# First block of a fused attention and expert kernel: state scaled by a kept copy, more load buffers, one unit issued later

## The chip, the core and the metric

The kernel runs on one core of a Trainium2 chip. The metric is the device time of one execution in microseconds (us); lower is better. In the profile TensorE is PE (matmul) and PEld (weight load), VectorE is DVE, ScalarE is ACT, GpSimd is POOL, and SyncE is SP, whose queue (SPq) issues nearly all DMAs here.

## What is computed

```python
f = 1 / (1 + exp(-f_logit))
for t in range(768):                      # 4 batches x 8 heads, head size 48
    state = f[t][:, None] * state + k[t] (outer) v[t]
    y[t] = q[t] @ state
x = y, heads side by side                 # 3072 tokens x 384
h = x @ w_in                              # 384 -> 2048
x = (h * clip(h + 3, 0, 6) / 6) @ w_out   # 2048 -> 384
e = argmax(x @ w_gate)                    # one of 8 experts for each token
out = gate * sigmoid(x @ w_output_gate)[e] * (relu(x @ w1[e]) @ w2[e])   # 384 -> 1024 -> 384
```

w_in and w_out arrive as 64-bit floats, the rest as 32-bit floats.

## The kernel before

Tokens are worked on in 8 blocks of 384. For each block four attention **units** (two batch-head pairs of a block of tokens each, `attention(blk, pr, xx)`) write a quarter of the tile `xx` that the first multi-layer product (`mlp`) of that block reads. A unit turns the recurrence into products: DVE runs two scans (`gg` L233, the running decay, and `r0` L235, its inverse) and four elementwise steps (`rg` L237, `kt` L238, `kb` L240, `qt` L242); PE transposes `kb` (`pk` L248) and multiplies (`pa` L253, `pkv` L266); DVE masks (`at` L260) and adds states (`st` L274 to L277 in the first half of a sequence, L281 in the second); ACT copies the states (`sbd` L284); PE multiplies again (`py` L291, L294); ACT and DVE write the result in two parts (L300, L301). The fourth unit of a block writes into `yx`, which six DMAs (L305) spread over `xx`; only then can the products `ph` of that block (L310 to L312) start.

`mlp` takes 16 hidden tiles f. For each it does nine products into `ph` (two PSUM buffers), the activation (ACT L347, DVE L348, ACT L349, DVE L350; the buffer of `ph` is free after L348), and two tiles later nine products into `acc` (L323 to L325).

Before and during block 0 the 64-bit weights are converted in 24 **parts** (`split64`): a DMA of 512 KB into `raw` (two buffers; the tile's name in the profile), then DVE L138, L140, ACT L143, DVE L144, ACT L145, DVE L146. Seven parts are issued between the units of block 0, the others two per hidden tile of block 0.

Which unit is issued where is set by `UNITS = (-5, 0, 5, 9)` and the function `between(f)`, called after each hidden tile f: the first unit of block 1 (the fifth unit) is issued ahead of block 0's `mlp`, the first unit of a later block at f = 11 two blocks ahead, the three others at f = 0, 5, 9 of the block ahead. Program order is only a priority: a scheduler with a timeline of its own sets the order of the instructions on each engine (last line of the file), and each engine then works strictly in that order, SP's queue of DMAs too. Eight products on zeros (`keep_warm`) stand in the units of block 0.

Buffers: `qt` and `xt` 3, `kt` 2, `vs` 2, `th`, `gg` and `r0` 1. A load into a buffer waits until its last reader is done. In program order `gg` of a unit is read last by L277, which scales the new state by the last column of `gg`; L244 copies the same column to `gcmin`.

After the last block the tokens are gathered by expert and run through eight experts (`up`, `down`, `rows_in`, `rows_out`); this part is not touched.

Of the kernel before, what the change touches and what calls it, by code (L numbers as in the profile page):

```python
# [10 lines left out]
F32 = mybir.dt.float32  # L11
F32R = mybir.dt.float32r
BF16 = mybir.dt.bfloat16
I32 = mybir.dt.int32
U32 = mybir.dt.uint32
# [7 lines left out]
P = 128  # L23
# [3 lines left out]
KD = DM // P  # L27
FF = 2048
NF = FF // P
# [3 lines left out]
TB = 384  # L33
NB = NT // TB
CH = 128
# [13 lines left out]
def fused(ctx: ExitStack, tc: tile.TileContext, q, k, fl, v, vt, w_in, w_out, wg, w1, w2, out):  # L49
# [79 lines left out]
    def split64(pool, hi, lo, src):  # L129

        raw = work.tile([P, SW // 2, 2], U32, tag="raw", name="raw64")
        loads.append(nc.sync.dma_start(out=raw.rearrange("p n t -> p (n t)"), in_=src))
        lw, hw = raw[:, :, 0], raw[:, :, 1]
# [18 lines left out]
    def load_first(pool, i, wih, wil, woh, wol):  # L152

        wohf, wolf = (t.rearrange("p f d -> p (f d)") for t in (woh, wol))

        def up(kt):
            sl = slice(i * 512, (i + 1) * 512)
            split64(pool, wih[:, kt, sl], wil[:, kt, sl], w_in.bitcast(U32)[:, kt, 1024 * i:1024 * (i + 1)])

        def down(j):  # L160
            sl = slice(j * 512, (j + 1) * 512)
            split64(pool, wohf[:, sl], wolf[:, sl], w_out.bitcast(U32)[:, 1024 * j:1024 * (j + 1)])

        return [partial(up, kt) for kt in range(KD)] + [partial(down, j) for j in range(3 * i, 3 * i + 3)]
# [47 lines left out]
    def attention(blk, pr, xx):  # L212
# [4 lines left out]
        kt = at2.tile([R, NCH, CH], F32, tag="kt", name="kt")  # L217
# [25 lines left out]
        gend = fl2(gg)[:, TB - 1:TB]  # L243
        nc.scalar.copy(gcmin[:, n:n + 1], gend)  # L244
# [17 lines left out]
        if blk == 0:  # L262
            keep_warm(1, fl2(kb))
# [4 lines left out]
        if blk == 0:  # L268
            keep_warm(1, fl2(kb))

        if half == 0:
# [5 lines left out]
            nc.vector.tensor_scalar_mul(state[pr][:, 0, :], st[:, 0, :], gend)  # L277
# [183 lines left out]
    parts = [part for i in range(NF // 4) for part in load_first(cv, i, *wfirst)]  # L461
# [5 lines left out]
    for pr in range(4):  # L467
        if UNITS[pr] < -1:
            att_unit(1, pr)
# [158 lines left out]
    for blk in range(NB):  # L628
# [11 lines left out]
        def between(f):  # L640
# [6 lines left out]
            for pr in range(4):  # L647
                if f == UNITS[pr] and blk + 1 < NB:
                    att_unit(blk + 1, pr)
                if f == UNITS[pr] + NF and blk + 2 < NB:  # L650
                    att_unit(blk + 2, pr)
# [64 lines left out]
    with tc.If(general > 0):  # L716
# [41 lines left out]
        with ExitStack() as es:  # L758
            gp = es.enter_context(tc.tile_pool(name="gw", bufs=1))
            wg1 = first_weights(gp)  # L760
            for i in range(NF // 4):
                for part in load_first(gp, i, *wg1):
                    part()
# [105 lines left out]
```

## Time and profile before

| | us |
|---|---|
| three runs | 864.46, 866.75, 869.58 |
| median | 866.75 |
| profiled execution | 864.98 |
| its span on the engines | 863.3 |
| PE busy in it | 805.9 (93%) |
| DVE busy in it | 526.4 (61%) |

The profiled execution is 1.77 us under the median, and its span leaves 1.7 us around it. PE is busy nearly all the time from about 75 us on. Before that, in the units of block 0, it mostly waits. The shares over the whole span hide that DVE is busy all the time in just this stretch. Matmuls overlap in the records: a row's time is 0.33 us at the full clock, but the next one starts 0.17 us later. DVE's rows overlap a little too, so the step from one start to the next is the price.

### The profile page before, as it was taken

Reading aid. Unit: us, or ns where it says so; the run is one execution under the profiler, and the core shown is the slowest. Engines: PE = TensorE matmul, PEld = TensorE weight load, DVE = VectorE, ACT = ScalarE, POOL = GpSimd, SP = SyncE. Lnnn points to the kernel's source line nnn. Section 1 sums busy time; section 2 is a strip of 40 time slices with the busy share of each in tenths; the row PEclk is TensorE's granted clock in tenths of the full one; section 3 lists DMA queues with packets and bytes.
Section 4 is the critical chain, followed back from the end, with each engine's and each line's share of the span. In section 5 each row is a group of like instructions: output and inputs, shape, how many; then the busy total and the mean of one; then the engine's idle time right before and its main releaser. Section 6 shows DMA issues by size and latency. Waiting matters only on the chain.

```text
span 863.3 us, 14521 instructions
## 1 busy us (share of the span) xinstructions
PE 805.9 (93%) x5503; PEld 746.4 (86%) x5503; DVE 526.4 (61%) x1118; ACT 396.4 (46%) x843; POOL 62.3 (7%) x103
## 2 busy tenths in 40 slices
PE   7558998999998999999899999999999999999995
PEld 3338987998997998999799899899898999999994
DVE  6999975569554578654567843463464452554631
ACT  5556654447434455633445533453354342453520
POOL 2000000200010010010010010010100011101111
PEclk9558999999999999999999999999999999999998
DMA  6565495023021113110211200050254163255600
GB/s 200 169 187 156 153 283 168 29 68 106 1 70 52 31 62 92 48 61 26 65 63 42 57 29 11 14 174 20 68 178 157 34 207 131 92 185 183 216 26 28
DMA packets 42412, 85.01 MB, mean 98 GB/s; under 512 B 5954, under 2 KB 29795, under 8 KB 42333
## 3 DMA queue, kind: packets, MB, share of 16 engines
q1 hardware_dynamic: 39052, 74.50, 28.5%
q0 software_dynamic: 3280, 9.49, 3.0%
q8 instruction: 45, 0.74, 0.4%
q14 instruction: 35, 0.28, 0.1%
HBM read 65.77 MB, written 16.26 MB: 95 GB/s over the span
## 4 chain that ended last, share of the span: by engine, by line
PE 47%; DVE 4%; DMA 3%; ACT 2%; issue 1%; SPq 0%; POOL 0%; POOLq 0%; DVEq 0%; ACTq 0%
PE ph L310 7%; PE ph L312 7%; PE ph L311 7%; PE acc L323 3%; PE acc L324 3%; PE acc L325 3%; PE yacc L311 2%; PE yacc L312 2%; PE yacc L310 2%; DMA raw<-in_w 2%; PE yrow L599 1%; PE yrow L595 1%; PE yrow L598 1%; PE px L553 1%; PE py L291 1%
## 5 line engine op out<-in xcount | busy, mean ns | idle before, releaser
L310 PE MATMUL ph<-xx,wih 128*128 128x384 f32 x384 | 134.0, 349 | 9.8 <-DMA xx<-yx 6.5
L312 PE MATMUL ph<-xx,wil 128*128 128x384 f32 x384 | 132.6, 345 | 0.0
L311 PE MATMUL ph<-xx,wih 128*128 128x384 f32 x384 | 131.9, 344 | 0.0
L347 ACT ACTIVATE gf<-ph,three 128x384 f32<-128x384 f32 x128 | 73.6, 580 | 126.1 <-PE ph L312 122.9
L324 PE MATMUL acc<-wol,gh 128*128 128x384 f32 x384 | 129.8, 338 | 0.0
L323 PE MATMUL acc<-woh,gh 128*128 128x384 f32 x384 | 129.4, 337 | 0.3 <-ACT gh L349 0.3
L325 PE MATMUL acc<-woh,gl 128*128 128x384 f32 x384 | 122.0, 337 | 0.0
L348 DVE SCALAR_TENSOR_TENSOR gf<-gf,ph 128x384 f32<-128x384 f32 x128 | 70.1, 551 | 80.8 <-ACT gf L347 80.0
L350 DVE TENSOR_TENSOR gl<-gf,gh 128x384 fp32r<-128x384 f32 x128 | 70.4, 552 | 34.8 <-ACT gh L349 34.2
L354 DVE SCALAR_TENSOR_TENSOR hl<-ph,hh 128x256 fp32r<-128x256 f32 (+7 forms) x72 | 39.0, 542 | 82.2 <-ACT hh L353 77.2
L349 ACT CAST gh<-gf 128x384 fp32r<-128x384 f32 x128 | 65.3, 512 | 51.2 <-DVE gf L348 49.5
L310 PEld LDWEIGHTS ph<-xx,wih 128*128 128x128 f32 x384 | 74.2, 193 | 13.6 <-DMA xx<-yx 7.3
L353 ACT ACTIVATE hh<-ph 128x256 fp32r<-128x256 f32 (+7 forms) x72 | 34.6, 481 | 109.3 <-PE ph L312 109.3
L312 PEld LDWEIGHTS ph<-xx,wil 128*128 128x128 f32 x384 | 74.0, 193 | 0.9 <-issue 0.5
L311 PEld LDWEIGHTS ph<-xx,wih 128*128 128x128 f32 x384 | 74.0, 193 | 0.3
L323 PEld LDWEIGHTS acc<-woh,gh 128*128 128x128 f32 x384 | 72.1, 188 | 1.1 <-ACT gh L349 0.6
L324 PEld LDWEIGHTS acc<-wol,gh 128*128 128x128 f32 x384 | 72.1, 188 | 1.1 <-issue 0.7
L325 PEld LDWEIGHTS acc<-woh,gl 128*128 128x128 f32 x384 | 71.2, 188 | 0.8 <-issue 0.3
L310 PE MATMUL ph<-xh,w1h 128*128 128x256 f32 (+7 forms) x216 | 71.9, 334 | 0.0
L311 PE MATMUL ph<-xl,w1h 128*128 128x256 f32 (+7 forms) x216 | 71.7, 333 | 0.0
L312 PE MATMUL ph<-xh,w1l 128*128 128x256 f32 (+7 forms) x216 | 71.5, 332 | 0.0
L436 POOL DMA_INDIRECT xs_d<-row,sli x24 | 24.4, 1019 | 558.6 <-DVE sli L431 406.7
(168 smaller groups left out, 1471.0 us busy)
## 6 DMA issues: line engine op xcount, KB each, us to landing
raw<-in_w SPq DMA_DIRECT2D x23, 512.0 KB, 6.1
raw<-in_w SPq DMA_DIRECT2D x30, 384.0 KB, 3.4
vs<-in_v SPq DMA_DIRECT2D x32, 192.0 KB, 2.5
raw<-in_w_in SPq DMA_DIRECT2D x12, 512.0 KB, 4.2
raw<-in_w_out SPq DMA_DIRECT2D x12, 512.0 KB, 3.7
xt<-in_fl SPq DMA_DIRECT2D x32, 168.0 KB, 3.1
kt<-in_k SPq DMA_DIRECT2D x32, 168.0 KB, 2.3
qt<-in_q SPq DMA_DIRECT2D x32, 168.0 KB, 2.6
```

Source lines behind the costliest of these rows:

```text
L310: nc.tensor.matmul(ps, lhsT=wh, rhs=xh, start=first, stop=False)
L311: nc.tensor.matmul(ps, lhsT=wh, rhs=xl, start=False, stop=False)
L312: nc.tensor.matmul(ps, lhsT=wl, rhs=xh, start=False, stop=last)
L323: nc.tensor.matmul(acc[t], lhsT=gh[:, ts_], rhs=w2h[:, f, :], start=f == 0, stop=False)
L324: nc.tensor.matmul(acc[t], lhsT=gh[:, ts_], rhs=w2l[:, f, :], start=False, stop=False)
L325: nc.tensor.matmul(acc[t], lhsT=gl[:, ts_], rhs=w2h[:, f, :], start=False, stop=f == nf - 1)
L347: nc.scalar.activation(gf, ph, AF.Relu, bias=three)
L348: nc.vector.scalar_tensor_tensor(out=gf, in0=gf, scalar=6.0, in1=ph, op0=ALU.min, op1=ALU.mult)
L349: nc.scalar.copy(gh, gf)
L350: nc.vector.tensor_tensor(out=gl, in0=gf, in1=gh.bitcast(F32), op=ALU.subtract)
L353: return (nc.scalar.activation(gh, ph, AF.Relu).ins, nc.vector.scalar_tensor_tensor(out=gl, in0=ph, scalar=0.0, in1=gh.bitcast(F32), op0=A ...
L354: nc.vector.scalar_tensor_tensor(out=gl, in0=ph, scalar=0.0, in1=gh.bitcast(F32), op0=ALU.max, op1=ALU.subtract).ins)
```

## The change

- L277 reads `gcmin[:, n:n + 1]`, ACT's copy, in place of the last column of `gg`.
- `kt` gets three buffers.
- Raw weights go round through four buffers: the two of before and the tiles `xTh` and `xTl`, which lie idle until the end of block 0.
- The two `keep_warm` calls in the units of block 0 go (eight products).
- A table `starts` replaces the test in `between`: the units of block 1 are issued at f = 0, 4, 8, 11 of block 0, those of block 2 at f = -1, 2, 5, 9 of block 1, and from block 3 on as before. So the fifth unit is issued in block 0, and the first unit of block 2 in block 1.
- The conversion in the branch that is not taken here gets a buffer function.

```diff
-        raw = work.tile([P, SW // 2, 2], U32, tag="raw", name="raw64")
-        loads.append(nc.sync.dma_start(out=raw.rearrange("p n t -> p (n t)"), in_=src))
-        lw, hw = raw[:, :, 0], raw[:, :, 1]
+    buffers = cycle([lambda: work.tile([P, SW], F32, tag="raw", name="raw").bitcast(U32)] * 2 + [
+        lambda n=n: rtp.tile([P, KD, TB], F32R, tag=n, name="raw", bufs=1).rearrange("p k t -> p (k t)").bitcast(U32)
+        for n in ("xTh", "xTl")])
+    def split64(pool, raw, hi, lo, src):
+        raw = raw[:, 0:SW]
+        loads.append(nc.sync.dma_start(out=raw, in_=src))
+        lw, hw = (raw.rearrange("p (n t) -> p n t", t=2)[:, :, i] for i in range(2))
...
-        kt = at2.tile([R, NCH, CH], F32, tag="kt", name="kt")
+        kt = at2.tile([R, NCH, CH], F32, tag="kt", name="kt", bufs=3)
...
-        gend = fl2(gg)[:, TB - 1:TB]
-        nc.scalar.copy(gcmin[:, n:n + 1], gend)
+        nc.scalar.copy(gcmin[:, n:n + 1], fl2(gg)[:, TB - 1:TB])
...
-        if blk == 0:
-            keep_warm(1, fl2(kb))
...
-        if blk == 0:
-            keep_warm(1, fl2(kb))
...
-            nc.vector.tensor_scalar_mul(state[pr][:, 0, :], st[:, 0, :], gend)
+            nc.vector.tensor_scalar_mul(state[pr][:, 0, :], st[:, 0, :], gcmin[:, n:n + 1])
...
     UNITS = (-5, 0, 5, 9)
+    starts = {(blk - 1, f) if f >= 0 else (blk - 2, f + NF): (blk, pr) for blk in range(3, NB) for pr, f in enumerate(UNITS)}
+    starts.update({(0, f): (1, pr) for pr, f in enumerate((0, 4, 8, 11))})
+    starts.update({(1, f): (2, pr) for pr, f in enumerate((-1, 2, 5, 9))})
...
-    for pr in range(4):
-        if UNITS[pr] < -1:
-            att_unit(1, pr)
...
-            for pr in range(4):
-                if f == UNITS[pr] and blk + 1 < NB:
-                    att_unit(blk + 1, pr)
-                if f == UNITS[pr] + NF and blk + 2 < NB:
-                    att_unit(blk + 2, pr)
+            if (blk, f) in starts:
+                att_unit(*starts[blk, f])
```

All the lines of the changed file from L138 to L260 of before stand four or five lines further down (L138 is L143, L140 is L145, L144 is L149, L146 is L151, L233 is L238, L235 is L240, L237 is L242, L238 is L243, L240 is L245, L242 is L247).

What the scheduler makes of it is seen at three places. The first is DVE just ahead of the write of `yx` by the fourth unit of block 0, on which the start of block 0's products hangs. Numbers tell the tiles apart; s64_ and r64_ are the conversion's tiles, the highest number the latest part. Before:

```order
L233 SCALAR_TENSOR_TENSOR gg_546<-th_545,zero_154 112x384
L138 TENSOR_SCALAR s64_742<-raw64_740 128x512
L237 TENSOR_TENSOR rg_554<-r0_547,gg_546 112x384
L242 TENSOR_TENSOR qt_537<-qt_537,gg_546 112x384
L146 TENSOR_TENSOR wol_165<-s64_732,woh_164 128x512
L140 SCALAR_TENSOR_TENSOR s64_742<-raw64_740,s64_742 128x512
L240 SCALAR_TENSOR_TENSOR kb_557<-rg_554,kt_538 112x384
L138 TENSOR_SCALAR s64_778<-raw64_776 128x512
L233 SCALAR_TENSOR_TENSOR gg_657<-th_656,zero_154 112x384
L144 ISA s64_742<-s64_742,r64_743 128x1024
L301 TENSOR_TENSOR yx_517<-py_506,yx_517 128x384
```

The same place after:

```order
L240 SCALAR_TENSOR_TENSOR r0_1207<-xt_1199,rmax_155 112x384
L145 SCALAR_TENSOR_TENSOR s64_707<-raw_705,s64_707 128x512
L276 TENSOR_TENSOR st_482<-st_482,pkv_475 112x48
L151 TENSOR_TENSOR wol_165<-s64_697,woh_164 128x512
L243 TENSOR_TENSOR kt_1198<-kt_1198,r0_1207 112x384
L149 ISA s64_707<-s64_707,r64_708 128x1024
L277 TENSOR_SCALAR st_483<-st_482,gcmin_133 112x48
L143 TENSOR_SCALAR s64_743<-raw_741 128x512
L145 SCALAR_TENSOR_TENSOR s64_743<-raw_741,s64_743 128x512
L151 TENSOR_TENSOR wil_163<-s64_707,wih_162 128x512
L149 ISA s64_743<-s64_743,r64_744 128x1024
L301 TENSOR_TENSOR yx_501<-py_490,yx_501 128x384
```

The write of `yx` is instruction 105 on DVE before and 127 after. Ahead of it stand 11 finished sums of the conversion (L144) before and 14 after, 5 scans L235 before and 8 after; the rows r0_1207 and kt_1198 belong to the eighth unit.

The second place is SP's queue where `yx` of block 1's last unit is spread over `xx` (xs_d is the buffer of rows for the experts, filled with padding once; vs and qt are loads of later units). Before:

```order
L479 DMA xs_d_72<-pad_73 128x3x388
L481 DMA xs_d_72<-pad_73 128x388
L223 DMA vs_1600<-in_v 128x384
L221 DMA qt_1787<-in_q 112x384
L305 DMA xx_536<-yx_1220 16x2x384 x6
```

After:

```order
L226 DMA qt_1492<-in_q 112x384
L226 DMA xt_2075<-in_fl 112x384
L226 DMA kt_1945<-in_k 112x384
L228 DMA vs_1495<-in_v 128x384
L226 DMA qt_1624<-in_q 112x384
L226 DMA xt_2374<-in_fl 112x384
L226 DMA kt_2074<-in_k 112x384
L226 DMA xt_2560<-in_fl 112x384
L228 DMA vs_1627<-in_v 128x384
L226 DMA qt_1771<-in_q 112x384
L305 DMA xx_566<-yx_1260 16x2x384 x6
```

Before, the spread stands two loads behind the padding; after, ten loads lie between the padding and the spread.

The third place is PE between the last unit of block 2 (py) and block 2's first product (ph). After, one piece:

```order
L291 MATMUL py_2000<-at_1974,vs_1947 64x128 x4
L294 MATMUL py_2000<-qt_1944,sbd1_160 64x128 x2
L291 MATMUL py_2000<-at_1974,vs_1947 64x128 x2
L294 MATMUL py_2000<-qt_1944,sbd1_160 64x128 x2
L252 MATMUL pk_2097<-ident_95,kb_2093 128x112 x3
L257 MATMUL pa1_2105<-qt_2073,kb_2093 128x128
L257 MATMUL pa0_2104<-qt_2073,kb_2093 128x128
```

Four more rows of pa, four of pkv and then the products of block 2 follow. Before, these stand ahead of block 2's first products:

```order
L323 MATMUL acc2_1579<-woh_164,gh_2216 128x384
L324 MATMUL acc2_1579<-wol_165,gh_2216 128x384
L325 MATMUL acc2_1579<-woh_164,gl_2217 128x384
L253 MATMUL pa1_2121<-qt_2089,kb_2109 128x128
L253 MATMUL pa0_2120<-qt_2089,kb_2109 128x128
```

There the py of that unit lies 40 rows further up, inside the last hidden tiles of block 1; after, it stands behind all of them.

## Rows read from the trace of the kernel before

**Rows 1.** The page's first part: busy time, share of the span, instructions of each engine.

```profile
PE 805.9 (93%) x5503; PEld 746.4 (86%) x5503; DVE 526.4 (61%) x1118; ACT 396.4 (46%) x843; POOL 62.3 (7%) x103
```

**Rows 2.** Stretches: length, busy PE, PEld, DVE, ACT, POOL, then granted clock, DMA share, GB/s.

```profile
64.40:75.30 10.90, 8.55 (x46) 7.93 (x46) 10.90 (x22) 7.52 (x17) 0.00 (x0) 0.66 0.57 160
75.30:100.00 24.70, 24.70 (x169) 23.85 (x168) 24.70 (x50) 16.36 (x36) 0.00 (x0) 0.98 0.51 151
```

**Rows 3.** The stretch before block 0's products, DVE alone: length, busy, clock, DMA, GB/s.

```profile
0.00:64.40 64.40, 55.26 (x111) 0.67 0.64 186
```

**Rows 4.** What DVE waited for up to 64.4: us, times, longest.

```profile
DVE gg L233 <- ACT th L230: 3.0, 1, 3.0
DVE at L260 <- PE pa L253: 2.1, 1, 2.1
DVE s L138 <- DMA raw<-in_w_in: 1.4, 1, 1.4
DVE zero L197 <- PEq L856: 1.0, 1, 1.0
```

**Rows 5.** DVE in order of time up to yx: start, time, instruction.

```profile
57.93 0.68 DVE L140 SCALAR_TENSOR_TENSOR s<-raw,s 128x512 uint32<-128x512 uint32 x1
58.53 0.54 DVE L240 SCALAR_TENSOR_TENSOR kb<-rg,kt 112x384 f32<-112x384 f32 x1
59.00 0.41 DVE L138 TENSOR_SCALAR s<-raw 128x512 uint32<-128x512 uint32 x1
59.34 0.94 DVE L233 TENSOR_TENSOR_SCAN gg<-th,zero 112x384 f32<-112x384 f32 x1
60.20 0.66 DVE L144 CUSTOM_DVE_ANT_0 s<-s,r 128x1024 uint16<-128x1024 uint16 x1
60.79 0.54 DVE L301 TENSOR_TENSOR yx<-py,yx 128x384 fp32r<-128x384 f32 x1
```

**Rows 6.** The start of block 0's products: start, time, instruction, idle before and its releaser.

```profile
61.36 3.94 SPq L305 DMA_DIRECT2D xx<-yx  x6
...
64.43 0.66 PE L310 MATMUL ph<-xx,wih 128*128 128x384 f32 x1 [0.75 <-DMA xx<-yx]
...
72.40 0.44 PE L291 MATMUL py<-at,vs 128*64 128x128 f32 x4 [2.32 <-ACT sbd L284]
...
75.30 0.67 PE L310 MATMUL ph<-xx,wih 128*128 128x384 f32 x1
```

**Rows 7.** The products on zeros: times of one, first and last start.

```profile
L69 PE MATMUL warm<-kb,pad x16: 486/730/1009, 9.0 to 45.8; 112*128 112x384 f32 x16
```

**Rows 8.** DMA issues up to 64.4: count, KB each, median us to landing.

```profile
qt<-in_q SPq DMA_DIRECT2D x7, 168.0 KB, 4.2
```

**Rows 9.** The end of block 0 and the start of block 1.

```profile
122.57 0.44 PE L310 MATMUL ph<-xx,wih 128*128 128x384 f32 x1 [0.96 <-DVE gf L348]
...
140.32 0.41 PE L310 MATMUL ph<-xx,wih 128*128 128x384 f32 x1 [2.58 <-DMA xx<-yx]
...
141.12 0.52 PE L311 MATMUL ph<-xx,wih 128*128 128x384 f32 x1
141.44 0.52 PE L312 MATMUL ph<-xx,wil 128*128 128x384 f32 x1
...
146.01 0.44 PE L310 MATMUL ph<-xx,wih 128*128 128x384 f32 x1 [0.42 <-DVE gf L348]
146.29 0.33 PE L311 MATMUL ph<-xx,wih 128*128 128x384 f32 x1
146.46 0.34 PE L312 MATMUL ph<-xx,wil 128*128 128x384 f32 x1
```

**Rows 10.** The start of block 3.

```profile
272.68 0.48 ACT L300 CAST yx<-py 128x384 fp32r<-128x384 f32 x1 [0.53 <-PE py L294]
273.85 0.94 PE L253 MATMUL pa<-qt,kb 48*128 48x128 f32 x12 [0.78 <-ACT kn L250]
276.72 0.41 PE L310 MATMUL ph<-xx,wih 128*128 128x384 f32 x1 [1.44 <-DMA xx<-yx]
```

More of the change, by code (lines that the diff above doesn't have):

```diff
@@ L127, in fused @@
     loads = []
-    def split64(pool, hi, lo, src):
-        raw = work.tile([P, SW // 2, 2], U32, tag="raw", name="raw64")
-        loads.append(nc.sync.dma_start(out=raw.rearrange("p n t -> p (n t)"), in_=src))
-        lw, hw = raw[:, :, 0], raw[:, :, 1]
+    buffers = cycle([lambda: work.tile([P, SW], F32, tag="raw", name="raw").bitcast(U32)] * 2 + [
[5 more added lines that the diff above has]
+        lw, hw = (raw.rearrange("p (n t) -> p n t", t=2)[:, :, i] for i in range(2))
         s = pool.tile([P, SW // 2], U32, tag="s64", name="s64", bufs=2)
@@ L150, in first_weights, with load_first @@
                                                           ("woh", [P, NF, DM]), ("wol", [P, NF, DM]))]
-    def load_first(pool, i, wih, wil, woh, wol):
+    def load_first(pool, raw, i, wih, wil, woh, wol):
         wohf, wolf = (t.rearrange("p f d -> p (f d)") for t in (woh, wol))
@@ L157, in up @@
             sl = slice(i * 512, (i + 1) * 512)
-            split64(pool, wih[:, kt, sl], wil[:, kt, sl], w_in.bitcast(U32)[:, kt, 1024 * i:1024 * (i + 1)])
+            split64(pool, raw(), wih[:, kt, sl], wil[:, kt, sl], w_in.bitcast(U32)[:, kt, 1024 * i:1024 * (i + 1)])
         def down(j):
             sl = slice(j * 512, (j + 1) * 512)
-            split64(pool, wohf[:, sl], wolf[:, sl], w_out.bitcast(U32)[:, 1024 * j:1024 * (j + 1)])
+            split64(pool, raw(), wohf[:, sl], wolf[:, sl], w_out.bitcast(U32)[:, 1024 * j:1024 * (j + 1)])
         return [partial(up, kt) for kt in range(KD)] + [partial(down, j) for j in range(3 * i, 3 * i + 3)]
@@ L460, in fused @@
     UNITS = (-5, 0, 5, 9)
-    parts = [part for i in range(NF // 4) for part in load_first(cv, i, *wfirst)]
+    starts = {(blk - 1, f) if f >= 0 else (blk - 2, f + NF): (blk, pr) for blk in range(3, NB) for pr, f in enumerate(UNITS)}
+    starts.update({(0, f): (1, pr) for pr, f in enumerate((0, 4, 8, 11))})
+    starts.update({(1, f): (2, pr) for pr, f in enumerate((-1, 2, 5, 9))})
+    parts = [part for i in range(NF // 4) for part in load_first(cv, lambda: next(buffers)(), i, *wfirst)]
     for pr, n in enumerate((0, 3, 3, 1)):
@@ L761, in fused @@
             for i in range(NF // 4):
-                for part in load_first(gp, i, *wg1):
+                for part in load_first(gp, lambda: gp.tile([P, SW], U32, tag="raw", name="raw"), i, *wg1):
                     part()
```

## The prediction

> **What bounds the kernel now.** I read the page's busy shares first. PE is busy for 805.9 us of a span of 863.3 [rows 1], so all that can be won or lost lies in some 57 us of waiting, apart from products at the lower clock. Next come the stretches. From 75.3 us on PE is busy all the time, 24.70 of 24.70 us up to 100, though DVE is full there too [rows 2]: DVE works just far enough ahead. Before that it is the other way round. In 64.4 to 75.3 DVE is busy for all 10.90 us and PE for 8.55 [rows 2], and up to 64.4 DVE is busy for 55.26 us [rows 3] while PE waits for what DVE hands it. So the head of the kernel is a queue of DVE work in fixed order, and the kernel ends a fixed amount of PE work after the moment at which PE becomes full. That moment is the third hidden tile's first product at 75.30 [rows 6]. The second and third places with a price are the handovers from block to block, where PE waits for the six DMAs that spread yx: 2.58 us at block 1, 1.44 at block 3 [rows 9, 10].
>
> The bound for "same" is 0.5% or 4.3 us, about what a measurement of this kernel can tell from no change.
>
> **The head, part by part.** The order on DVE says what the change does there; the trace gives the prices. In rows that follow each other without a gap, the step from start to start is 0.60 us for L140, 0.59 for L144 (I take 0.60 for both and for L146, whose tile has the same size as L140's), 0.34 for L138, 0.86 for the scan L233 (L235 is the same scan with other operands) and 0.47 for an elementwise step such as L240 [rows 5].
>
> Ahead of the write of yx stand 22 more DVE instructions than before: 2 of L138, 3 each of L140, L144 and L146, 4 scans, 7 elementwise steps. That is 2 x 0.34 + 9 x 0.60 + 4 x 0.86 + 7 x 0.47 = 12.8 us. The fifth unit, issued later in the program, is not later on DVE: its scans and its kb still precede that write, and its pk, pa and pkv still precede block 0's products on PE. What has moved forward with it are three parts of the conversion, and scans and key steps of units six to eight, which the third kt buffer lets in.
>
> The later landmark counts more. PE gets full when the fifth unit's py is done (it starts at 72.40 after a wait for sbd), because the third hidden tile stands behind it [rows 6]. That sbd needs the second L281 of the fifth unit. Ahead of it stand 18 more instructions: 3 of L138, 10 of L140, L144 and L146, 2 scans, 3 elementwise: 3 x 0.34 + 10 x 0.60 + 2 x 0.86 + 3 x 0.47 = 10.1 us.
>
> Against this stand DVE's own waits. Up to 64.4 DVE is idle for 64.40 - 55.26 = 9.1 us [rows 3]. Of these 4.0 lie at the very start, before the first data and the first tanh [rows 4], and stay. The other 5.1 can go: 2.1 for the first pa, which the second unit's scan now covers (this is what the kept copy of the decay does: gg comes free early), 1.4 for raw, which four buffers cover, the rest small [rows 4]. L277 now waits for a copy that ACT makes right after the scan, long before: no cost.
>
> New waits come in. The multiplication of qt of the fifth, sixth and seventh unit now stands on DVE one or two rows behind the write of the result (L301) of the second, third and fourth. Its load needs the qt buffer that just this unit's py reads last (three buffers), and SP issues it, behind vs, when py ends. ACT and DVE need about 1 us for the result, the load 4.2 to landing [rows 8]; so DVE may wait up to 3 us, three times, with conversions and yx queued behind. Where DVE comes late anyway it waits for nothing. I take 3.0 in all, between 0 and 9.
>
> The head then is +10.1 - 5.1 + 3.0 = **+8.0 us**, with +5.0 (no new wait) and +14 (all of them) as ends. It cannot come out below +5.0 unless DVE's steps get shorter, for which no row gives a reason.
>
> The products on zeros cost nothing either way: the granted clock was 0.67 on the mean over the head and 0.66 while block 0's products begin [rows 2, 3], so for much of it at the lower of its two levels, 1.2 GHz, though they are issued up to 45.8 us [rows 7]. They stand on PE, which waits for DVE there. If the cover goes, they save at most 0.5 to 1.0 us each on PE [rows 7].
>
> The rows give the raw loads 1.4 us of DVE's idle time [rows 4]. The Trainium skill (Perfetto Trace Analysis, Optimization Strategy) says that gaps which repeat on the engine that should be full can mean too few buffers. By that rule the whole 5.1 us would be the buffers' doing and the head would end nearer +5.0; by the rows they are three different waits, only one of them for raw.
>
> **The handovers.** At block 1 PE lost 0.96 us at 122.57 (DVE held up by a late load), 2.58 at 140.32 for the spread of yx, which SP issued behind the padding, then ran 11 products with the clock at its lower level, at steps of 0.32 (141.12 to 141.44) instead of 0.17 (146.29 to 146.46), which is 1.6, and lost 0.42 at 146.01 [rows 9]: 5.6 in all. After, the padding is queued earlier, since the last part is loaded earlier, and ten loads lie between. From ACT's copy of the last py to the first product the spread takes 4.0 us at block 3, 272.68 to 276.72 [rows 10]; in the new order 23 products of 0.17, 3.9 us, lie between. I leave 0.4 of the 5.6: **-5.2**. The ends: -5.6, and 0 if one of the ten loads holds the spread up as the padding did.
>
> At block 2 some 40 products lay between, 40 x 0.17 = 6.8 us, more than the spread's 4.0. Now the py of its last unit is the last thing but pk, pa and pkv. This is the pattern of block 3, 0.78 + 1.44 = 2.2 us [rows 10]; if the clock falls as at block 1, up to 1.6 more. I take **+2.5**, ends +1.4 and +3.8.
>
> The units moved by a hidden tile or two inside blocks 0 and 1 change nothing where PE is full. PE's own work is the same but for the eight products. From block 3 on the program is as before.
>
> **Sum.** 8.0 - 5.2 + 2.5 = +5.3 us on the profiled execution's 864.98, so 870.3. That execution was 1.8 under the median of the three runs; against 866.75 the sum is **872.0**.
>
> **Rivals.** First, slower by far: the new waits for qt all come, and the spread at block 1 waits in SP's queue behind vs_1627 and qt_1771. The head is +11 to +14, the handover gains 2 or 3: +11 or more, 878 and up. For it: DMA took 4.2 us to landing in the head [rows 8]. Against: DVE is late at two of the three places by my count. It decides from 6 us of new waits on. 17%.
>
> Second, the same: DVE runs without new waits, +5.0, and both handovers go as summed: +5.0 - 5.2 + 2.2 = +2, 869. For it: the raw loads now run three parts ahead, so that the queue is less crowded when qt comes. 26%.
>
> Third, faster: the fifth unit's work really leaves the head. Its two scans and four elementwise steps are 2 x 0.86 + 4 x 0.47 = 3.6 us of DVE. If they, and not the conversions, set the moment at which PE gets full, the head is -3.6, the handovers -5.2 + 2.5: -6.3, 860.5. It decides as soon as the parts ahead of yx cost nothing, that is, if PE is held by the units' chain and not by DVE's count. Against: DVE has no gap ahead of yx [rows 5], and the order keeps the unit ahead. The Trainium skill (Perfetto Trace Analysis, Optimization Strategy) says that interleaving stretches with different bottlenecks can help; that is what this rival would be. 12%. That the change does not do what its words say, the fifth unit staying in the head, is part of the forecast.
>
> **How the numbers follow.** The forecast (+1 to +9, centre +5.3) has 45%, the rivals 17, 26 and 12. Of the forecast about four fifths lie above +4.3. Slower: 0.36 + 0.17 = 0.53 of which I keep 0.52; same: 0.09 + 0.26 = 0.35; faster: 0.12, and 0.01 for what I don't see. The range 865 to 879.5 holds the forecast and the second rival and half of the first; it leaves out the third and the far end of the first.
>
> **What the profile after would show.** Right: the write of yx near 69 to 71 us (60.79 before), block 0's first product near 72 to 74 (64.43), the third hidden tile's first product near 82 to 84 (75.30); no wait over 0.6 us at block 1 and no clock loss there; a new wait of about 2 us at block 2. Wrong: block 0's products start before 66, or waits for qt on DVE are absent or above 6 us, or PE has gaps in block 0 after 84 that DVE's backlog causes, which I price at nothing.

## The result, and the profile after

The changed kernel takes 870.36 us (median of 18 runs, 868.9 to 875.0), the kernel before 864.73 (18 runs on the same chips). The ratio is 1.0062 with a 95% interval of 1.0048 to 1.0077: 5.6 us slower, beyond the 0.5% that the prediction named. The prediction had +5.3 us and 872.0. Its 872.0 stands higher than 870.4 since the three runs known then had a median of 866.75; on the profiled execution of before (864.98) its sum was 870.3, and the profiled execution of after took 870.80.

PE's busy time and the stretch answer to [rows 1, 2]; the first line is the page's, the other a window of the kernel after (length, then busy time of PE, PEld, DVE, ACT, POOL, granted clock, DMA share, GB/s).

```profile
PE 795.8 (92%) x5487; PEld 742.0 (85%) x5487; DVE 524.7 (60%) x1118; ACT 396.7 (46%) x843; POOL 59.6 (7%) x103
...
83.80:869.00 785.20, 758.67 (x5213) 713.80 (x5213) 449.38 (x968) 350.62 (x740) 55.12 (x68) 0.99 0.28 87
```

From the third hidden tile's first product to the end the kernel after needs 785.20 us, the kernel before 863.3 - 75.30 = 788.0. So the head lost 83.80 - 75.30 = 8.5 us and the rest gained 2.8. These are the landmarks of the head (kernel after, order of time; columns as in [rows 6]):

```profile
70.77 0.55 DVE L301 TENSOR_TENSOR yx<-py,yx 128x384 fp32r<-128x384 f32 x1
71.34 4.80 SPq L305 DMA_DIRECT2D xx<-yx  x6
75.91 0.66 PE L310 MATMUL ph<-xx,wih 128*128 128x384 f32 x1 [2.24 <-DMA xx<-yx]
79.89 0.20 DVE L281 TENSOR_TENSOR st<-st,pkv 112x48 f32<-112x48 f32 x1
81.34 0.44 PE L291 MATMUL py<-at,vs 128*64 128x128 f32 x4 [0.24 <-ACT sbd L284]
83.80 0.45 PE L310 MATMUL ph<-xx,wih 128*128 128x384 f32 x1 [0.48 <-DVE gf L348]
```

The write of yx comes at 70.77 instead of 60.79 [rows 5], and the fifth unit's second L281, on which its py waits, ends the count of DVE's work for the head. (The third tile itself waits last, for 0.48 us, for DVE's L348, which stands behind that L281 in DVE's order; it starts 3.9 us after the L281 here and 3.8 in the kernel before.) Up to there DVE is busy for 62.36 of 71.50 us in the kernel before (window of DVE alone: length, busy, clock, DMA share, GB/s):

```profile
0.00:71.50 71.50, 62.36 (x125) 0.67 0.65 186
```

and for 71.42 of 79.90 us in the kernel after, in the same window of DVE:

```profile
0.00:79.90 79.90, 71.42 (x143) 0.59 0.71 203
```

That is 18 instructions and 9.1 us of work more, and 0.7 us less of waiting (9.1 before, 8.5 after). What DVE waits for has changed, though. The two largest waits of the kernel after up to 85 us (us, times, longest) answer to [rows 4]:

```profile
DVE gg L238 <- ACT th L235: 3.9, 2, 3.0
DVE qt L247 <- DMA qt<-in_q: 3.4, 4, 1.1
```

Three of the four for qt, as rows of DVE in order of time:

```profile
42.00 0.56 DVE L247 TENSOR_TENSOR qt<-qt,gg 112x384 f32<-112x384 f32 x1 [1.13 <-DMA qt<-in_q]
57.41 0.56 DVE L247 TENSOR_TENSOR qt<-qt,gg 112x384 f32<-112x384 f32 x1 [1.12 <-DMA qt<-in_q]
72.64 0.56 DVE L247 TENSOR_TENSOR qt<-qt,gg 112x384 f32<-112x384 f32 x1 [0.99 <-DMA qt<-in_q]
```

The waits for pa (2.1), raw (1.4), ACT's halves of the weights (0.9) and its half of a result (0.2) are gone; 3.4 for qt and 0.9 for a second tanh have come. Three waits for qt of about 1.1 us stand exactly where the prediction looked for them.

At block 1 nearly nothing is lost any more; the first rows answer to [rows 9] (kernel after):

```profile
138.80 3.78 SPq L305 DMA_DIRECT2D xx<-yx  x6
141.69 0.41 PE L310 MATMUL ph<-xx,wih 128*128 128x384 f32 x1 [0.20 <-DMA xx<-yx]
143.44 0.55 PE L366 MATMUL px<-ident,row 128*128 128x128 f32 x3 [0.46 <-ACT row L363]
```

0.20 + 0.46 = 0.7 us is left of 5.6. At block 2, where the kernel before had one wait of 1.01 us (for sbd, at 210.93), the kernel after has three, and its clock falls:

```profile
208.01 0.66 PE L291 MATMUL py<-at,vs 128*64 128x128 f32 x8 [0.74 <-ACT sbd L284]
210.55 0.94 PE L257 MATMUL pa<-qt,kb 48*128 48x128 f32 x12 [0.78 <-ACT kn L254]
213.43 0.66 PE L310 MATMUL ph<-xx,wih 128*128 128x384 f32 x1 [1.58 <-DMA xx<-yx]
...
215.81 0.52 PE L311 MATMUL ph<-xx,wih 128*128 128x384 f32 x1
216.13 0.47 PE L312 MATMUL ph<-xx,wil 128*128 128x384 f32 x1
216.44 0.34 PE L310 MATMUL ph<-xx,wih 128*128 128x384 f32 x1
216.61 0.33 PE L311 MATMUL ph<-xx,wih 128*128 128x384 f32 x1
```

Nine products run at steps of 0.32 instead of 0.17, which is 1.4 us; with 0.74 + 0.78 + 1.58 that makes 4.5, or 3.4 more than before.

To follow a kernel through the program, take the first product of block 2's hidden tile f = 10 (f counts from 0) as a ruler: but for one kernel, named below, the same number of PE's instructions lies between the third tile and it, and its start, less that of before, says how far a kernel is behind. The kernel after is 6.8 us behind there: 8.5 from the head, -4.9 at block 1, +3.4 at block 2, which sum to 7.0.

### The profile page after: what moved, and what is told of

It is laid out like the page before. It is cut to its first block, busy times and chain, and to the rows that moved or that the text cites. A ratio compares the mean times of both kernels' runs of the same rounds, so it can differ in the third digit from the quotient of the medians.

```text
span 869.0 us, 14493 instructions
## 1 busy us (share of the span) xinstructions
PE 795.8 (92%) x5487; PEld 742.0 (85%) x5487; DVE 524.7 (60%) x1118; ACT 396.7 (46%) x843; POOL 59.6 (7%) x103
## 4 chain that ended last, share of the span: by engine, by line
PE 77%; DMA 8%; DVE 7%; ACT 3%; issue 2%; SPq 1%; POOL 0%; POOLq 0%; ACTq 0%; DVEq 0%
PE ph L310 11%; PE ph L312 11%; PE ph L311 11%; PE acc L323 7%; PE acc L324 7%; PE acc L325 7%; PE py L291 3%; DMA qt<-in_q 3%; PE yacc L311 3%; PE yacc L310 3%; PE yacc L312 3%; PE pa L257 2%; PE py L294 2%; DMA xt<-in_fl 1%; PE yrow L599 1%
## 5 line engine op out<-in xcount | busy, mean ns | idle before, releaser
L348 DVE SCALAR_TENSOR_TENSOR gf<-gf,ph 128x384 f32<-128x384 f32 x128 | 69.9, 549 | 57.7 <-ACT gf L347 57.4
L291 PE MATMUL py<-at,vs 128*64 128x128 f32 x384 | 39.1, 299 | 31.3 <-ACT sbd L284 31.3
```

The source lines that it names most:

```text
L291: products += [nc.tensor.matmul(o, lhsT=vs[:, c, x, :], rhs=at[:, x, c, :], start=True, stop=first) for x, o in halves]
L348: nc.vector.scalar_tensor_tensor(out=gf, in0=gf, scalar=6.0, in1=ph, op0=ALU.min, op1=ALU.mult)
```

## The experiments

All kernels compute the whole reference. Third tile: start of the third hidden tile's first product, in the profiled execution. Ruler: block 2's tile f = 10 against the kernel before. Span: of the profiled execution. The median is of 18 runs for the kernels before and after and of 4 to 10 for the others; the ratio is to the kernel before on the same chip, and since the chips differ, it is the ratios and not the medians that can be held against each other. Executions of one kernel differ by some 2 us either way (the kernel before ran from 861 to 870), so that a single trace shows places and mechanisms, and the ratios show sizes.

| kernel | third tile | ruler | span | median | ratio (95%) |
|---|---|---|---|---|---|
| before | 75.30 | 0 | 863.3 | 864.73 | 1 |
| after | 83.80 | +6.8 | 869.0 | 870.36 | 1.0062 (1.0048 to 1.0077) |
| after, old state line | 72.63 | -1.7 | 862.6 | 863.60 | 0.9993 (0.9969 to 1.0018) |
| before, new state line | 85.50 | +8.2 | 869.9 | 871.29 | 1.0052 (1.0031 to 1.0074) |
| before, two gg | 80.80 | +2.0 | 860.4 | 862.79 | 0.9980 (0.9953 to 1.0007) |
| before, four raw | 73.10 | -6.7 | 856.1 | 858.39 | 0.9932 (0.9911 to 0.9953) |
| before, new table | 77.79 | +2.9 | 868.0 | 865.96 | 1.0002 (0.9983 to 1.0021) |
| before, four raw and new table | 74.77 | +0.8 | 862.5 | 865.87 | 1.0009 (0.9988 to 1.0030) |
| after, two raw | 83.71 | +7.8 | 868.7 | 872.86 | 1.0111 (1.0073 to 1.0148) |
| after, two kt | 83.86 | +6.4 | 870.8 | 870.15 | 1.0068 (1.0043 to 1.0093) |
| after, two kt, four qt | 81.64 | +9.2 (see there) | 867.1 | 869.00 | 1.0062 (1.0044 to 1.0079) |
| after, products on zeros | 85.15 | +7.1 | 867.2 | 868.27 | 1.0047 (1.0028 to 1.0067) |
| after, block 2's units back | 83.84 | +4.7 | 868.1 | 869.72 | 1.0058 (1.0037 to 1.0079) |
| after, old state line, block 2's units back | 74.39 | -2.8 | 860.7 | 864.16 | 0.9996 (0.9982 to 1.0009) |

**Which part moves the head?** The prediction put the scans and key steps that moved ahead of yx down to the third key buffer, and gave no cause of its own for the parts of the conversion; the four raw buffers are the obvious one. The order of the instructions says otherwise once the parts are taken apart: with two raw buffers, with two for keys or with the products on zeros, DVE's order up to the fifth unit's second L281 keeps its 143 rows; with the old state line alone it falls back to 125. So that line was undone in the kernel after, and made alone in the kernel before.

```
 # after, old state line
+        gend = fl2(gg)[:, TB - 1:TB]
-            nc.vector.tensor_scalar_mul(state[pr][:, 0, :], st[:, 0, :], gcmin[:, n:n + 1])
+            nc.vector.tensor_scalar_mul(state[pr][:, 0, :], st[:, 0, :], gend)
```

> The changed kernel with one part undone: the state of the first units is again scaled by the last column of gg itself, not by the kept copy. Theory A: this line alone had brought the head's new order about, since the third and fourth unit's scan may overwrite gg early only without that late reader. The order on DVE ahead of the fifth unit's second L281 falls from 70.1 to 60.0 us of work (143 to 125 rows, priced by the pitches of the prediction), the 3.2 us of waits for qt go, the 2.1 us for pa come back; the third hidden tile's first product comes at 74 to 76 (83.80 in the changed kernel), and the whole is 7 to 9 us below the changed kernel: 862 to 863, 2 to 3 below the kernel before. Theory B (the prediction's own attribution): the conversions moved forward by the four raw buffers and the scans let in by the third kt buffer are the cause: third tile stays at 82 to 84, time 869 to 871.

Measured: 863.60, third tile at 72.63, 11.2 us ahead of the kernel after, earlier than either theory said. The waits for qt are gone and the one for pa is back (a window of DVE up to the second L281 with its count of rows, then DVE and PE, kernel after with the old state line):

```profile
0.00:69.65 69.65, 62.53 (x125) 0.63 0.72 208
12.21 1.02 DVE L265 TENSOR_TENSOR at<-pa,nmask 128x384 f32<-128x384 f32 x2 [1.45 <-PE pa L258]
72.63 0.67 PE L311 MATMUL ph<-xx,wih 128*128 128x384 f32 x1
201.72 1.65 PE L258 MATMUL pa<-qt,kb 48*128 48x128 f32 x12 [2.37 <-ACT row L364]
204.58 0.66 PE L311 MATMUL ph<-xx,wih 128*128 128x384 f32 x1 [0.60 <-DMA xx<-yx]
```

Theory A holds for the head. In the whole, only some 6 us of the 11 remain (ratio 0.9993 against 1.0062): at block 2 PE now waits 2.37 for pa and 0.60 for the spread.

```
 # before, new state line
-            nc.vector.tensor_scalar_mul(state[pr][:, 0, :], st[:, 0, :], gend)
+            nc.vector.tensor_scalar_mul(state[pr][:, 0, :], st[:, 0, :], gcmin[:, n:n + 1])
```

> The kernel before with that one line alone: the state is scaled by the kept copy of the decay; buffers, products on zeros and the table of units as before. Theory A: the whole loss of the head comes with it: third hidden tile's first product at 82.5 to 84.5 (75.30 before), about 3 us of waits of DVE for qt, and 6 to 9 us slower than before, 871 to 874, as the handover to block 1 is not mended. Theory B: without the extra buffers it moves next to nothing, at best the 2.1 us of DVE's wait for pa are gone: 862 to 865.

Measured: 871.29, third tile at 85.50. This one line makes the kernel before as slow as the whole change does, as far as the intervals can tell. DVE has its 143 rows up to the second L281, and waits for raw and for qt (window and rows of DVE, then PE):

```profile
0.00:80.50 80.50, 71.69 (x143) 0.62 0.64 187
14.93 0.43 DVE L138 TENSOR_SCALAR s<-raw 128x512 uint32<-128x512 uint32 x1 [2.18 <-DMA raw<-in_w_in]
57.95 0.56 DVE L242 TENSOR_TENSOR qt<-qt,gg 112x384 f32<-112x384 f32 x1 [1.50 <-DMA qt<-in_q]
85.50 0.44 PE L310 MATMUL ph<-xx,wih 128*128 128x384 f32 x1 [1.04 <-DVE gf L348]
```

**Is it the copy, or gg coming free early?** With the old line gg is held until the unit's state is scaled, after its pkv. With the new one it is free as soon as rg, qt and ACT's copy have read it, and the next unit's scans may go ahead. A second gg buffer frees it as early, without the copy.

```
 # before, two gg
-        gg = at1.tile([R, NCH, CH], F32, tag="gg", name="gg")
+        gg = at1.tile([R, NCH, CH], F32, tag="gg", name="gg", bufs=2)
```

> The kernel before with a second buffer for gg, and the state still scaled by gg itself: gg comes free early without the kept copy. Theory A: what moves the head is that the next units' scans may run early, by whatever means; the order ahead of the fifth unit's second L281 rises from 60.0 to 68.8 us of DVE (125 to 140 rows), the third hidden tile comes at 82 to 84.5 (75.30 before), with 1.5 to 3.5 us of waits for qt. 62 products now lie between block 0's last result and block 1's first product, so that this handover's 5.6 us may go; the whole 866 to 869 (864.7 before). Theory B: it is the new reader of ACT's copy in L277 that holds DVE, not the early scans: third tile at 75 to 76, and 859 to 862.

Measured: third tile at 80.80, 862.79. The order moves nearly as with the kept copy (140 rows), so the early release moves it, not the copy. The head loses 5.5 us and not 8.5: no row of DVE waits for qt before 85 us, and 1.06 us for raw (at 76.39) is the largest wait behind the first tanh.

```profile
80.80 0.44 PE L310 MATMUL ph<-xx,wih 128*128 128x384 f32 x1 [1.15 <-DVE gf L348]
```

So the moved work, less the waits that it covers, costs some 5 us without any wait for qt, as the prediction's own lower end of the head (+5.0, "no new wait") had it; the 3 us up to the kernel after fit its 3.4 of waits for qt, though the two kernels also differ by three rows. The whole came out 3 to 6 us below what was expected, and no slower than the kernel before: at block 1 PE no longer waits for the spread, which is issued as soon as yx is written (134.65), long after the padding's last issue (122.95), and from the third tile to the ruler this kernel gains 3.5 us. The early release costs the head; whether it costs the whole depends on what the later start does to the handovers.

**What do the raw buffers and the table give?** Each was put alone into the kernel before.

```
 # before, four raw
+    buffers = cycle([lambda: work.tile([P, SW], F32, tag="raw", name="raw").bitcast(U32)] * 2 + [
+        lambda n=n: rtp.tile([P, KD, TB], F32R, tag=n, name="raw", bufs=1).rearrange("p k t -> p (k t)").bitcast(U32)
+        for n in ("xTh", "xTl")])
```

> The kernel before with four buffers for raw weights alone. In the order the head is row for row the old one up to the fifth unit's second L281 (125 rows, 60.0 us). Theory A: DVE's wait of 1.45 us for raw goes, the third tile comes 1 to 3 us earlier (72.5 to 74.3), and with 60 products between block 0's last result and block 1's first product (6 before) the 5.6 us lost there go too: 857.5 to 860.5. Rival: the spread of yx still stands behind the padding in SP's queue, or block 2 loses what block 1 gains, as in the run with the state's line undone: 862 to 864.5.

Measured: 858.39, 0.9932 (0.9911 to 0.9953), faster than both kernels. The third tile comes at 73.10: DVE waits for raw no more, and the fifth unit's py runs at steps of 0.22 where it ran at 0.43. At block 1 the loss is 0.33 us (SP, with DVE's write of yx between, then PE):

```profile
123.07 0.91 SPq L485 DMA_DIRECT2D xs_d<-pad  x1
123.95 0.55 DVE L305 TENSOR_TENSOR yx<-py,yx 128x384 fp32r<-128x384 f32 x1
126.66 5.52 SPq L309 DMA_DIRECT2D xx<-yx  x6
133.30 0.41 PE L314 MATMUL ph<-xx,wih 128*128 128x384 f32 x1 [0.33 <-DMA xx<-yx]
200.21 0.41 PE L314 MATMUL ph<-xx,wih 128*128 128x384 f32 x1 [0.30 <-DMA xx<-yx]
```

The padding is queued behind the last raw load, 16 issues about 1.05 us apart, and this last load has moved: the padding's first and last issue stand at 107.09 and 123.07 here, at 97.76 and 113.52 in the kernel after, at 114.33 and 130.15 in the kernel before, where the spread followed at 133.12. These are the rows of before that belong beside it (DVE, then SP):

```profile
126.67 0.55 DVE L301 TENSOR_TENSOR yx<-py,yx 128x384 fp32r<-128x384 f32 x1
133.12 6.38 SPq L305 DMA_DIRECT2D xx<-yx  x6
```

In the kernel before yx is written at 127.2 and its spread is issued 5.9 us later; with four raw buffers it is written at 124.5, and the spread follows 2.2 us later. So the padding still holds the spread up, only less: from the last py of that unit to block 1's first product it is 14.4 us before, 10.1 here and 4.4 in the kernel after. PE has 72 instructions of other work in these 10.1 us, and only 0.33 is left over to wait.

```
 # before, new table
+    starts.update({(0, f): (1, pr) for pr, f in enumerate((0, 4, 8, 11))})
+    starts.update({(1, f): (2, pr) for pr, f in enumerate((-1, 2, 5, 9))})
...
+            if (blk, f) in starts:
+                att_unit(*starts[blk, f])
```

> The kernel before with the new table of units alone: fifth unit issued in block 0, block 2's units later; old state line, two raw and two key buffers, products on zeros kept. In the order the head is the old one (125 rows, 60.0 us), 36 products lie ahead of block 1 (6 before) and 58 ahead of block 2 (42). Theory A: third tile at 75 to 76, the loss at block 1 gone (4.5 to 5.6 us), none at block 2: 859 to 861. Rival: PE waits at block 2 for kn, sbd or row, which ACT delivers late, 2 to 5 us: 862 to 865.

Measured: 865.96, no change (1.0002). Neither theory: the loss at block 1 stays, though 36 instructions of PE lie between. The padding's last issue is at 133.83, and with two loads behind it it holds the spread in SP's queue for 1.9 us after yx is written (SP, with DVE's write between, then PE):

```profile
133.83 1.01 SPq L481 DMA_DIRECT2D xs_d<-pad  x1
134.54 0.56 DVE L301 TENSOR_TENSOR yx<-py,yx 128x384 fp32r<-128x384 f32 x1 [0.80 <-ACT yx L300]
137.02 5.38 SPq L305 DMA_DIRECT2D xx<-yx  x6
143.69 0.66 PE L310 MATMUL ph<-xx,wih 128*128 128x384 f32 x1 [2.27 <-DMA xx<-yx]
```

From the last py to the first product it is 9.7 us, nearly what it is with four raw buffers (10.1). There 72 instructions of PE fill the time; here there are only 36, and PE waits 2.27 us.

The two together tell what the table costs when the buffers have done their part:

```
 # before, four raw and new table: both diffs above
```

> The kernel before with four raw buffers and the new table of units, nothing else, to be held against the one with four raw buffers alone (858.4). In the order the head is the old one; ahead of block 2 lie 23 products instead of 38, ahead of block 1 24 instead of 60. Theory A: the table costs at block 2 what it cost with the state's line undone (waits of 2.37 and 0.60 us and a clock drop, 4.9 us on the ladder), and brings nothing at block 1, whose loss the raw buffers had already ended: 862 to 864.5. Rival: block 2's loss came from the third key buffer or the missing products on zeros: 857.5 to 860.

Measured: 865.87 (1.0009), against 858.39 (0.9932) with the buffers alone. From the third tile to the ruler the kernel without the table gains 4.5 us on the kernel before, the one with it loses 1.3. The place is mainly block 2, as theory A had it (another 1.2 us are eight products at the lower clock right behind the third tile); the key buffer and the products on zeros are not in this kernel, so they are not its cause. Twelve products behind these rows run at steps of 0.32 (PE):

```profile
204.02 1.61 PE L257 MATMUL pa<-qt,kb 48*128 48x128 f32 x12 [2.37 <-ACT row L367]
206.89 0.66 PE L314 MATMUL ph<-xx,wih 128*128 128x384 f32 x1 [0.67 <-DMA xx<-yx]
```

The reverse, two raw buffers in the kernel after:

```
 # after, two raw
-    buffers = cycle([lambda: work.tile(...)] * 2 + [lambda n=n: rtp.tile(...) for n in ("xTh", "xTl")])
+    buffers = cycle([lambda: work.tile([P, SW], F32, tag="raw", name="raw").bitcast(U32)])
```

> The changed kernel with two raw buffers instead of four. In the order of DVE the head stays the changed one (143 rows, 70.1 us ahead of the fifth unit's second L281). Theory A: the four buffers are worth in the head the waits for raw they cover (2.9 us with two buffers in the kernel before with the kept copy), and they bring the padding forward, which follows the last raw load in SP's queue (from 97.76 on in the changed kernel, 107 to 118 in those with two): third tile at 84.5 to 86.5, padding from 104 to 112 on, block 1 still nearly without a wait since the padding ends before 129; time 871 to 874. Rival: the raw loads are hidden by the waits for qt, third tile within 0.7 us of 83.80 and time 869.5 to 871.

Measured: 872.86, but of four runs with a wide interval. The trace gives the head to the rival: third tile at 83.71, in spite of one wait of 1.15 us for raw just ahead of it, and 1.85 us for qt in one place. The padding starts at 105.27, and block 1 waits 1.31 us (DVE and PE below). In the changed order, then, this one trace shows no gain of the head from the raw buffers; what they are worth in the whole there stays open.

```profile
59.08 0.56 DVE L245 TENSOR_TENSOR qt<-qt,gg 112x384 f32<-112x384 f32 x1 [1.85 <-DMA qt<-in_q]
143.89 0.41 PE L308 MATMUL ph<-xx,wih 128*128 128x384 f32 x1 [1.31 <-DMA xx<-yx]
```

**Block 2.** Its units were issued where they were, first in the kernel after, then with the old state line as well.

```
 # after, block 2's units back
-    starts.update({(1, f): (2, pr) for pr, f in enumerate((-1, 2, 5, 9))})
+    starts.update({(0, 12): (2, 0), (1, 0): (2, 1), (1, 5): (2, 2), (1, 9): (2, 3)})
```

> The changed kernel with block 2's four units issued where they were before, but for the first, which goes one place later (hidden tile 12 of block 0 instead of 11, which block 1's last unit holds). Theory A: the loss at block 2's start (waits of 0.74, 0.78 and 1.58 us and nine products at the lower clock) goes, 2.5 to 4 us, and block 1 stays nearly without a wait: 866.5 to 868 against 870.4. Rival, from the run with both parts undone, where block 2 came only 1.1 us earlier for it: PE waits for this unit's kn and sbd instead, and the gain is 0 to 1.5 us, 869 to 870.5.

> Both of these undone in the changed kernel: state scaled by gg itself, block 2's units back. Theory A: the two add up, -8 and -3 against 870.4: 858.5 to 861, 4 to 6 us faster than the kernel before (what is left of the change is the gain at block 1's start). Rival: head and handover trade against each other, since an earlier head brings the padding and the loads of block 1 back onto the spread of yx; then 862 to 865.

Measured: 869.72 and 864.16, neither to be told from the same kernel without this edit (870.36 and 863.60). The ruler shows a gain of 2.1 us in the one and 1.1 in the other. PE still waits there, 0.78 for pa and 1.56 for the spread in the first kernel; and by block 5 the first has given its 2 us back. The rivals come closer than theory A. Issuing a unit earlier in the program does not undo the loss; the kernel with four raw buffers alone, whose block 2 has the old units and 0.80 + 0.30 + 0.48 us of waits, does.

**The three small parts.** Key buffers, query buffers and the products on zeros:

```
 # after, two kt
-        kt = at2.tile([R, NCH, CH], F32, tag="kt", name="kt", bufs=3)
+        kt = at2.tile([R, NCH, CH], F32, tag="kt", name="kt")
 # after, two kt, four qt: this, and
-        qt = at2.tile([R, NCH, CH], F32, tag="qt", name="qt", bufs=3)
+        qt = at2.tile([R, NCH, CH], F32, tag="qt", name="qt", bufs=4)
 # after, products on zeros: the removed lines put back
+        if blk == 0:
+            keep_warm(1, fl2(kb))
```

> The changed kernel with two buffers for keys instead of three. The order on DVE up to the fifth unit's second L281 is the same row for row (143 rows, 70.1 us), so the prediction's sentence that the third buffer lets scans and key steps of later units in is already doubtful. Theory A: the keys now land later, as their buffer comes free later, but never last: third tile at 83.5 to 84.8, time 870 to 871.5. Rival: the key load becomes a new wait of DVE in each of units five to seven, 1 to 3 us more: 871.5 to 874.

> The changed kernel with two buffers for keys and four for queries (there is no room for three and four), to be held against the one with two for keys. A unit's query then no longer waits until the py three units earlier has read it. Theory A (the prediction's third term): DVE's three waits of 1.1 us for qt go, 3.2 us in all; the order puts 1.4 us more of DVE's work ahead of the fifth unit's second L281 (146 rows, 71.5 us), so the third tile comes 1.5 to 3 us earlier than with three, at 81 to 82.5, time 867.5 to 869.5. Rival: the wait only changes its name, to the landing of raw or kt behind it in the same queue: within 1 us of the run with two key buffers.

> The changed kernel with the eight products on zeros back. Theory A (the prediction's): they gain and cost nothing, since PE waits for DVE there and the clock is at its lower level all the same: third hidden tile's first product at 83.4 to 84.2 (83.80 without them), time 869.5 to 871.3. Theory B: they keep the clock up in the units' chains, which DVE and ACT then wait less for: third tile 1 to 3 us earlier, time 867.5 to 869.5.

Measured: with two key buffers nothing moves (third tile 83.86, ratio 1.0068), as theory A had it. With a fourth query buffer the waits for qt shrink to 0.24 us twice and the third tile comes 2.2 us earlier than with three, as expected (kernel after with two kt and four qt, the first of the two rows of DVE, then PE):

```profile
41.25 0.56 DVE L247 TENSOR_TENSOR qt<-qt,gg 112x384 f32<-112x384 f32 x1 [0.24 <-DMA qt<-in_q]
81.64 0.45 PE L310 MATMUL ph<-xx,wih 128*128 128x384 f32 x1 [0.83 <-DVE gf L348]
209.49 0.94 PE L257 MATMUL pa<-qt,kb 48*128 48x128 f32 x12 [1.86 <-ACT kn L254]
```

But the ratio is 1.0062, no better: the 2.2 us are gone again at the ruler, and at block 7's tile f = 10 the two kernels are level (588.02 and 587.89). PE's wait of 1.86 us for kn at block 2 is one place; where the rest goes is not shown. (This is the kernel whose ruler doesn't compare: 27 more of PE's instructions, the py and pk of a unit of the next block, stand ahead of it and take 1.7 us, so that its +9.2 is some +7.5.) The products on zeros leave the third tile 1.4 us later and the ratio lower (1.0047 against 1.0062), with overlapping intervals. That they save something is open; that they shorten the head, theory B, is not what the trace shows.

**Do the parts add up?** The kernel before with four raw buffers and the table stands at 1.0009, the state's line alone adds 0.0052, together 1.0061; the whole change has 1.0062. So the third key buffer and the missing products on zeros are left with nothing that these intervals (some 0.002 either way) could tell.

## Why the prediction was right, point by point

The time, the sign and the three terms were right; the cause behind the largest term was not. The terms came out 0.5, 0.3 and 0.9 us above the forecast, 1.7 in all, and most of it was given back from block 3 on, which the prediction put at nothing: that the sum fits within half a microsecond is in part luck.

- **The head, +8.0.** Measured +8.5. Its parts: 10.1 us more work of DVE, measured 9.1; waits that go, 5.1, measured 4.6 (pa 2.1, raw 1.4, the rest 1.1), and 0.9 us of new waiting for a tanh that was not foreseen; new waits for qt 3.0, measured 3.4, in the three places named. Two runs bear the split out, each with an order of its own (140 and 146 rows): with no wait for qt the head lost 5.5 (two gg), with 0.5 us of them 6.3 (four qt).
- **Why the work moved ahead: wrong.** The step "What has moved forward with it are three parts of the conversion, and scans and key steps of units six to eight, which the third kt buffer lets in" failed. With two key buffers or two raw buffers the 143 rows stay. The state's line moves them: it lets gg go early, and the scheduler then fills DVE with the next units' scans and with more conversions ahead of the steps that PE needs first. The prediction counted that line as the gain of 2.1 us for pa. That gain came, inside a change of order that cost 10.
- **The raw buffers, 1.4 us.** Mis-sized. Alone they bring the third tile 2.2 us forward and leave 0.33 us of the wait at block 1; in the changed order the one trace with two raw buffers shows no gain of the head from the other two. The Trainium skill (Perfetto Trace Analysis, Optimization Strategy) says that repeated gaps on the engine that should be full can mean too few buffers. Here it held for the raw weights in the kernel before (0.9932). In the kernel after a third buffer for keys (1.0068 without, 1.0062 with) and a fourth for queries (1.0068 without, 1.0062 with) brought nothing that could be told.
- **The handover at block 1, -5.2.** Measured -4.9. Of its two reasons, padding queued earlier and products in between, neither stands alone. What counts is when the padding ends against yx, and how much PE has to do meanwhile: with the new table alone the spread is held for 1.9 us, 36 instructions lie between, and 2.27 us of waiting and the clock's fall are left; with four raw buffers alone it is held for 2.2 us, but 72 lie between, and 0.33 is left; in the kernel after the padding's last issue, at 113.52, lies 25 us ahead of the spread, and 23 products cover all but 0.20.
- **The handover at block 2, +2.5.** Measured +3.4, inside its ends of 1.4 and 3.8: py is last, the spread is waited for, and the clock falls, which the prediction had priced as its far end. It named one new wait of about 2 us; there are three, 3.1 us in all. That the table does this is shown by the pair with four raw buffers.
- **From block 3 on, 0.** Not so in detail. The ruler goes from +6.8 in block 2 to +9.8 in block 3 and +7.7, +8.2, +6.4 in blocks 4 to 6. In block 3 the waits of [rows 10] come again, with 1.01 for sbd ahead of them and 0.98 for xTh behind, and this time the clock falls; at blocks 4 and 6 waits of before (0.80, 0.34, 0.49; 1.20) are gone. It sums to about -1 us. That the scheduler orders these blocks differently was in the order of instructions and was left out of the working.
- **The products on zeros, 0.** Not contradicted: 1.0047 with them against 1.0062 without, intervals overlapping.
- **The signs.** The write of yx at 70.77 (69 to 71 named), the third tile at 83.80 (82 to 84), no wait over 0.6 at block 1 and no fall of the clock there, waits for qt present: right. Block 0's first product came at 75.91 and not at 72 to 74, since the six issues of the spread took 4.80 us (3.94 before) and PE waited 2.24 for it; the third tile did not hang on that.
- **The rivals.** "Faster", the fifth unit leaving the head, did not come: the new table alone gives 1.0002. "The same" needed DVE without new waits; 3.4 us for qt came. "Slower by far" needed 6 us of waits for qt; they stayed at 3.4.

## What to carry to other kernels

A buffer that comes free earlier is no gain by itself: it cost the head 5.5 us with a second gg buffer, which left the whole unchanged (0.9980, 0.9953 to 1.0007), and 10.2 with the state's line (1.0052). With a scheduler that fills an engine's queue by what is ready, it lets later iterations' work in ahead of what the bottleneck is waiting for. Before costing a change of several parts, build each part alone and see in the order of instructions which of them moves rows; here one short line did, and the key and raw buffers, which looked like the cause, did not. Then keep only the part that pays: the four raw buffers alone, without the state's line and the table, give 858.39 us, 0.7% below the kernel before.

## What the runs showed of the hardware

- A row of bulk DMAs on one queue delays the small ones behind it: 16 fills about 1.05 us apart hold SP for some 16 us. The six small DMAs that PE waits for, right behind them and two or three loads, are then issued over 5.4 to 6.4 us instead of 3.8, and block 1's first product starts 6.6 to 7.2 us after the first of them instead of 2.9 (138.80 to 141.69 in the kernel after).
- The granted clock does not fall after every wait of the same length. At block 3 of the kernel before, waits of 0.78 us for pa and 1.44 for the spread [rows 10] left it at its upper level, 2.4 GHz. At block 5, in the same execution, waits of 0.78 and 1.41 were followed by nine products at the lower, 1.2 GHz (windows of PE behind the two waits: length, busy, granted clock, DMA share, GB/s; then the row of block 5):

```profile
276.70:277.90 1.20, 1.18 (x6) 1.00 0.41 78
414.40:417.40 3.00, 3.00 (x10) 0.50 0.29 57
414.38 0.66 PE L310 MATMUL ph<-xx,wih 128*128 128x384 f32 x1 [1.41 <-DMA xx<-yx]
```

  Nor does one wait more decide it. In the kernel after, block 3 has 1.01 us for sbd ahead of 0.78 and 1.45, and the clock falls for ten products; block 5 has 1.16 for sbd ahead of 0.78 and 1.41, and it stays up (the same windows for the kernel after, then rows of block 5):

```profile
284.60:287.80 3.20, 3.20 (x10) 0.51 0.41 90
423.30:425.50 2.20, 2.18 (x11) 1.00 0.37 69
417.68 0.44 PE L291 MATMUL py<-at,vs 128*64 128x128 f32 x4 [1.16 <-ACT sbd L284]
423.26 0.41 PE L310 MATMUL ph<-xx,wih 128*128 128x384 f32 x1 [1.41 <-DMA xx<-yx]
```

  So a short wait can cost more than itself (nine products at steps of 0.32 instead of 0.17 are 1.4 us), or nothing more, and these runs do not show what decides it. Gains of 2 us at one place of this kernel were often lost at the next handover.
